# The up projections of a bilinear FFN as 7 block products instead of 8, with 15 block additions on VectorE

## The chip, the cores and the metric

One core of a Trainium2 chip runs the whole program. The metric is the device time of one execution in microseconds (us). The kernel before was run three times: 1170.25, 1170.40 and 1171.97 us, median 1170.4 us.

## The reference

Two stages. A routing attention over 4 batch elements, 8 heads, 768 positions, head size 64: each query and key is put into one of 16 clusters, scores between different clusters are masked, then softmax and a product with `v`. Its output, laid out as 3072 tokens by 512, goes through a bilinear FFN:

```python
x = attn_out.transpose(0, 2, 1, 3).reshape(B * S, H * D)   # 3072 x 512
a = x @ w_a                                                # 512 x 1536
b = x @ w_b                                                # 512 x 1536
return (a * b @ w_out).astype(np.float32)                  # 1536 x 512
```

## The kernel before, in words

Everything is float32 on TensorE except the one-hot masks. The program is one hand-written order of work: `short_path` runs 99 groups `g`, six for each pair of heads (16 pairs `p`, four for each batch element), and each engine takes its instructions in that order. A group does two key tiles of 128: `score` (L405; mask L413 and scores L422 on TensorE, exponential on ScalarE L429), `add_up` of the previous group (L433; row sums `acc`, L443, on VectorE for the first element, later mostly on GpSimd), `weigh` of the previous group (L448; product with `v`, L454), one step of preparing the next pair (`prep_steps`, L378; the assignment to clusters, `prep_assign`, is five VectorE operations from L345 to L356), and every third group `denominators` (L465). Later `normalize` (L483) takes the reciprocals of one half of 384 queries (three VectorE operations, L488) and multiplies `xT` by them on GpSimd (L490).

The FFN runs between, as filler, from the deque `ffn`. `ffn_block` (L502) makes the pieces of one block of 384 tokens (half an element): for each of 12 slices `f` of 128 hidden columns, `piece_a` multiplies the four 128-row chunks of `w_a` with `xT` (L510) and ScalarE copies the result out (L521); `piece_b` does the same with `w_b` and VectorE multiplies the two into `h` (L525). Then three `down` pieces of 12 matmuls of 512 columns (L531), a copy on ScalarE and a store from SP's queue. Each group adds `PER_GROUP` (L564) to a credit, and pieces are taken, at their cost in columns, until it is used up. `ffn_ready` puts a block in when its half is normalized. What is left after group 98 runs without attention beside it (`some_ffn`, L641).

The PSUM pool `ps_m` has three buffers, shared by FFN pieces, `denominators` and the preparation of the next pair; `ps_s` (scores) and `ps_o` (product with `v`) are apart. The weights come in as float64 and are rounded to float32 in 36 parts of 128 x 512 (`round_w`, L245: VectorE, ScalarE and GpSimd), parts 8 to 35 from group 23 on at 1.75 a group (`due`, L572).

Of the kernel before, what the change touches and what calls it, by code (L numbers as in the profile page):

```python
# [8 lines left out]
FP32 = mybir.dt.float32  # L9
# [21 lines left out]
P = 128  # L31
# [4 lines left out]
def kernel(  # L36
# [26 lines left out]
    csb = const.tile([P, D], FP32)  # L63
    nc.scalar.dma_start(out=csb, in_=centroids.rearrange("h c d -> (h c) d"))
# [4 lines left out]
    }  # L69

# [13 lines left out]
    cn = const.tile([P, 2, D], FP32)  # L84

# [4 lines left out]
    def centroids_in():  # L90

        nc.scalar.activation(out=ce, in_=one, func=AF.Sqrt)
        csq = const.tile([P, D], FP32)
# [21 lines left out]
        for a in range(2):  # L115
            nc.vector.tensor_scalar(out=cn[:, a, :], in0=csb,
                                    scalar1=crinv[:, 0:1], scalar2=None,
                                    op0=ALU.mult)
# [19 lines left out]
def short_path(nc, tc, ctx, c, cn, centroids_in, casts, n_far, q, k, v,  # L138
# [26 lines left out]
    denp = pool("denp", 1)  # L165
    xtp = pool("xtp", 2)
    hp_ = pool("hp", 2)
    hap = pool("hap", 2)
# [117 lines left out]
    def centroids_across():  # L286
        ps = ps_m.tile([P, 512], FP32, name="m")
        nc.tensor.transpose(out=ps[:, 0:P], in_=cn.rearrange("p a d -> p (a d)"),
# [52 lines left out]
    def prep_assign(ps):  # L341
        NG = 24
        sim = ps[:, 0:NG * NC].rearrange("p (g c) -> p g c", c=NC)
        mx = small.tile([P, NG], FP32, name="mx")
        nc.vector.tensor_reduce(out=mx, in_=sim, axis=AX.X, op=ALU.max)  # L345
        rk = simp.tile([P, NG, NC], FP32, name="sim")
        nc.vector.tensor_tensor(  # L347
            out=rk, in0=sim, in1=mx[:, :, None].broadcast_to((P, NG, NC)),
            op=ALU.is_ge)
        nc.vector.tensor_tensor(  # L350
            out=rk, in0=rk, in1=rank[:, None, :].broadcast_to((P, NG, NC)),
            op=ALU.mult)
        first = small.tile([P, NG], FP32, name="first")
        nc.vector.tensor_reduce(out=first, in_=rk, axis=AX.X, op=ALU.max)
        oh = oh_all.rearrange("p n (a e) -> p (n a) e", a=2)
        nc.vector.tensor_tensor(  # L356
            out=oh[:, :, 0:NC], in0=rk,
            in1=first[:, :, None].broadcast_to((P, NG, NC)), op=ALU.is_equal)
# [19 lines left out]
    def prep_steps(p):  # L378
# [3 lines left out]
        def both(*fs):  # L382
# [5 lines left out]
            lambda: prep_assign(prep_across(p)),  # L388
# [7 lines left out]
    unchecked = []  # L396
    UPP = 2 * NJ
# [67 lines left out]
    def denominators(p, hf):  # L465
# [3 lines left out]
        terms = [accs.pop((p, hf))]  # L469
# [7 lines left out]
        den = denp.tile([P, HB], FP32, name="den")  # L477
# [22 lines left out]
    ffn = deque()  # L500

    def ffn_block(b, blk):  # L502
# [25 lines left out]
        def down(n):  # L528
            ps = ps_m.tile([P, 512], FP32, name="m")
            for f in range(NF):  # L530
# [3 lines left out]
            y = wtp.tile([P, DM], FP32, name="rest")  # L534
            nc.scalar.copy(out=y, in_=ps)  # L535
            rows = out[b * S:(b + 1) * S, :].rearrange(
                "(p j) n -> p j n", j=NJ)[:, 3 * blk + n, :]
            nc.sync.dma_start(out=rows, in_=y)
# [5 lines left out]

    blocks = {}

    def ffn_ready(b, blk):

        ups, downs = blocks[b, blk] = ffn_block(b, blk)
        if b > 0:  # L550
            ffn.extend(ups + downs)
        elif blk == 0:
            ffn.extend(ups[0:8])
        else:
            ups0, downs0 = blocks[b, 0]
# [8 lines left out]
    PER_GROUP = (2 * NF * NCH * HB + 3 * NF * DM) * 2 // (HP * GPP)  # L564
    EARLY = HP * GPP + 1
# [5 lines left out]
    for i in range(8, len(w_parts)):  # L571
        due.setdefault(23 + int((i - 8) / 1.75), []).append(i)  # L572
# [11 lines left out]
    prep_assign(prep_across(0))  # L584
    for w in (1, 0):
        prep_onehot(0, w)
    for g in range(NG + 3):
# [27 lines left out]
        round_next()  # L615
        if ffn:
# [14 lines left out]
        if g <= EARLY:  # L631
            first, second = 4, 1
        else:
            first, second = 5, 3 if g < NG else 2
# [253 lines left out]
```

## Time and profile before

| | |
|---|---|
| median of three runs | 1170.4 us |
| the profiled execution | 1171.77 us |
| its span, first to last instruction | 1170.0 us |
| mean granted TensorE clock | 0.997 |
| TensorE busy | 1151.0 us, 98% of the span |
| VectorE, ScalarE, GpSimd busy | 396.3, 335.9, 256.1 us |

The profile is one execution. Busy times are sums of instruction durations on an engine; the chain of waits goes back from the last instruction to what released each step; a granted clock of 1.00 is TensorE's 2.4 GHz. Matmul durations are modelled and overlap, so the cost of one is read from the distance between starts.

### The profile page before, as it was taken

Reading aid. Unit: us, or ns where it says so; the run is one execution under the profiler, and the core shown is the slowest. Engines: PE = TensorE matmul, PEld = TensorE weight load, DVE = VectorE, ACT = ScalarE, POOL = GpSimd, SP = SyncE. Lnnn points to the kernel's source line nnn. Section 1 sums busy time; section 2 is a strip of 40 time slices with the busy share of each in tenths; the row PEclk is TensorE's granted clock in tenths of the full one; section 3 lists DMA queues with packets and bytes.
Section 4 is the critical chain, followed back from the end, with each engine's and each line's share of the span. In section 5 each row is a group of like instructions: output and inputs, shape, how many; then the busy total and the mean of one; then the engine's idle time right before and its main releaser. Section 6 shows DMA issues by size and latency. Waiting matters only on the chain.

```text
span 1170.0 us, 11898 instructions
## 1 busy us (share of the span) xinstructions
PE 1151.0 (98%) x4755; PEld 576.3 (49%) x4755; DVE 396.3 (34%) x614; ACT 335.9 (29%) x608; POOL 256.1 (22%) x245
## 2 busy tenths in 40 slices
PE   6999999999999999999999999999999999999998
PEld 3444555555544455544555445554455545554553
DVE  4899777577611212221122212122211221200100
ACT  4666433434223232312223132321322211100000
POOL 1111243444422132222212122121221321000000
PEclk8999999999999999999999999999999999999999
DMA  5322233322102010010101001010000000000000
GB/s 139 101 77 77 90 95 104 99 82 92 47 18 59 18 41 1 12 39 18 41 1 41 9 18 41 1 41 10 32 1 1 1 18 9 1 1 26 1 1 29
DMA packets 60782, 44.91 MB, mean 38 GB/s; under 512 B 48432, under 2 KB 53040, under 8 KB 60720
## 3 DMA queue, kind: packets, MB, share of 16 engines
q1 hardware_dynamic: 59744, 42.21, 12.5%
q10 hardware_dynamic: 976, 1.87, 0.5%
q8 instruction: 39, 0.64, 0.2%
q14 instruction: 23, 0.19, 0.1%
HBM read 37.78 MB, written 6.29 MB: 38 GB/s over the span
## 4 chain that ended last, share of the span: by engine, by line
PE 94%; DVE 4%; issue 1%; POOL 1%; DMA 0%; ACT 0%; DVEq 0%; POOLq 0%; ACTq 0%
PE m L510 41%; PE m L531 21%; PE O L454 11%; PE s L422 10%; PE s L413 3%; PE m L474 3%; PE m L309 2%; PE m L325 1%; PE m L366 1%; PE m L336 1%; DVE den L488 0%; DVE acc L443 0%; DVE sim L347 0%; DVE mx L345 0%; POOL wo_sb L269 0%
## 5 line engine op out<-in xcount | busy, mean ns | idle before, releaser
L510 PE MATMUL m<-xT,wa_sb 128*128 128x384 f32 x768 | 265.0, 488 | 1.3 <-ACT ohT L371 0.9
L510 PE MATMUL m<-xT,wb_sb 128*128 128x384 f32 x768 | 265.6, 489 | 0.0
L531 PE MATMUL m<-wo_sb,h 128*128 128x512 f32 x576 | 251.9, 595 | 0.0
L443 POOL TENSOR_TENSOR acc<-acc,pt 128x384 f32<-128x384 f32 x144 | 146.8, 1033 | 266.9 <-ACT pt L429 263.2
L525 DVE TENSOR_TENSOR h<-ha,m 128x384 f32<-128x384 f32 x96 | 53.2, 554 | 443.1 <-PE m L510 443.1
L510 PEld LDWEIGHTS m<-xT,wb_sb 128*128 128x128 f32 x768 | 143.9, 190 | 107.1 <-issue 9.6
L510 PEld LDWEIGHTS m<-xT,wa_sb 128*128 128x128 f32 x768 | 143.7, 190 | 105.4 <-issue 7.1
L429 ACT ACTIVATE pt<-s 128x768 f32<-128x768 f32 x192 | 145.3, 809 | 109.3 <-PE s L422 72.6
L531 PEld LDWEIGHTS m<-wo_sb,h 128*128 128x128 f32 x576 | 108.0, 190 | 137.1 <-issue 135.4
L521 ACT COPY ha<-m 128x384 f32<-128x384 f32 x96 | 45.9, 478 | 366.9 <-PE m L510 366.9
L454 PE MATMUL O<-pt,v 128*64 128x384 f32 x768 | 144.8, 499 | 0.0
L422 PE MATMUL s<-qkT 64*128 64x384 f32 x768 | 140.8, 486 | 0.0
L443 DVE TENSOR_TENSOR acc<-acc,pt 128x384 f32<-128x384 f32 x96 | 76.7, 828 | 158.9 <-POOL acc L443 158.5
L490 POOL TENSOR_TENSOR xT<-xT,den 128x384 f32<-128x384 f32 x32 | 33.8, 1057 | 255.6 <-DVE den L488 241.0
L454 PEld LDWEIGHTS O<-pt,v 128*64 128x64 f32 x768 | 46.6, 136 | 86.5 <-issue 84.1
L422 PEld LDWEIGHTS s<-qkT 64*128 64x128 f32 x768 | 71.1, 189 | 32.0 <-issue 0.6
L535 ACT COPY rest<-m 128x512 f32<-128x512 f32 x24 | 14.1, 585 | 250.3 <-PE m L531 250.3
L488 DVE RECIPROCAL den<-den 128x128 f32<-128x128 f32 x96 | 82.2, 911 | 3.6 <-ACT den L479 3.5
L413 PE MATMUL s<-ohT 64*128 64x384 bf16 x384 | 48.2, 329 | 0.7 <-DVE ohT L374 0.7
L443 DVE TENSOR_TENSOR acc<-pt 128x384 f32<-128x384 f32 x40 | 30.2, 772 | 51.7 <-ACT pt L429 51.7
L443 POOL TENSOR_TENSOR acc<-pt 128x384 f32<-128x384 f32 x24 | 27.2, 1134 | 45.7 <-ACT pt L429 45.7
L309 PE MATMUL m<-ident,qk 128*128 128x128 f32 x192 | 28.5, 289 | 6.7 <-DVE nfar L281 6.7
(84 smaller groups left out, 507.0 us busy)
## 6 DMA issues: line engine op xcount, KB each, us to landing
raw<-in_moe_w_out_dram SPq DMA_DIRECT2D x12, 512.0 KB, 3.2
out_dram<-rest SPq DMA_DIRECT2D x24, 256.0 KB, 2.0
qk<-in_q_dram SPq DMA_DIRECT2D x30, 192.0 KB, 3.8
qk<-in_k_dram SPq DMA_DIRECT2D x30, 192.0 KB, 4.1
v<-in_v_dram SPq DMA_DIRECT2D x15, 384.0 KB, 4.3
raw<-in_moe_w_a_dram SPq DMA_DIRECT2D x11, 512.0 KB, 3.5
raw<-in_moe_w_b_dram SPq DMA_DIRECT2D x11, 512.0 KB, 3.5
raw<-in_moe_w_a_dram ACTq DMA_DIRECT2D x1, 512.0 KB, 4.2
```

What stands on the lines that cost most here:

```text
L309: nc.tensor.transpose(out=ps[:, n * P:(n + 1) * P], in_=qks[p][:, w, j].rearrange("p a d -> p (a d)"), identity=ident)
L413: nc.tensor.matmul(out=s[:, a, 0:HB], lhsT=ohTs[p][r, S + j * P:S + (j + 1) * P], rhs=ohTs[p][r, hf * HB:(hf + 1) * HB], start=True, stop= ...
L422: nc.tensor.matmul(out=s[:, a, 0:HB], lhsT=qkTs[p][r, S + j * P:S + (j + 1) * P], rhs=qkTs[p][r, hf * HB:(hf + 1) * HB], start=False, stop ...
L429: nc.scalar.activation(out=pt, in_=s[:, :, 0:HB], func=AF.Exp, scale=SCALE)
L443: eng.tensor_tensor(out=acc[:, a, :], in0=probs[u - 1][:, a, :] if j == 1 else acc[:, a, :], in1=probs[u][:, a, :], op=ALU.add)
L454: nc.tensor.matmul(out=O_of[0][a * D:(a + 1) * D, 0:HB], lhsT=vs[p][:, a, j, :], rhs=probs[u][:, a, :], start=(j == 0), stop=(j == NJ - 1))
L474: nc.tensor.matmul(out=ps[a * D:(a + 1) * D, 0:HB], lhsT=ones, rhs=t[:, a, :], start=(n == 0), stop=(n == len(terms) - 1))
L488: nc.vector.reciprocal(out=part, in_=part)
L510: nc.tensor.matmul(out=ps[:, 0:HB], lhsT=w_sb[:, ch, f * P:(f + 1) * P], rhs=xTs[b][:, ch, t0:t0 + HB], start=(ch == 0), stop=(ch == NCH - 1))
L521: nc.scalar.copy(out=box["a"], in_=ps[:, 0:HB])
L525: nc.vector.tensor_tensor(out=box["h"][:, f, :], in0=box["a"], in1=ps[:, 0:HB], op=ALU.mult)
L531: nc.tensor.matmul(out=ps, lhsT=box["h"][:, f, n * P:(n + 1) * P], rhs=wo_sb[:, f, :], start=(f == 0), stop=(f == NF - 1))
```

## The change

For batch elements 1 to 3 both up projections are done by one level of Strassen's algorithm in the form with 15 additions. The 512 rows of `xT` and the 1536 hidden columns are each cut in two, and so are the 768 tokens; where eight block products stood there are seven. For each slice `i` of 6 and each of `w_a`, `w_b` there is a set: seven products `p1`, `p6`, `p2`, `p7`, `p4`, `p5`, `p3` of two matmuls each (128 x 128 weights, 384 tokens), four combinations S1 to S4 of weight blocks (eight VectorE operations of 128 x 128, in `half_1` and `half_2`), a copy of `p1` on ScalarE and seven VectorE additions that read PSUM. Four combinations of `xT` blocks (`combine_x`, eight VectorE operations of 128 x 384 per element) are made when the halves are normalized, one of them in place. The product with `a` moves to GpSimd (`done`, four per `w_b` set). Work space is that of the weight rounding, which is over by then. Element 0 keeps `ffn_block`.

Around it: a `todo` deque spreads the five operations of `prep_assign` and the three reciprocals of `normalize` between FFN pieces, one behind each; `normalize` stands ahead of the pieces of its group and `ffn_ready` behind them; the reciprocals are taken in `acc[:, 0, :]` and not in a tile of their own; the credit is 3813 a group until group 51 and 4224 after, where it was 4608; parts of the weight rounding fall due at 1.5 a group. An element's FFN now waits for both of its halves, so that of element 3 begins behind group 98. The centroids' tiles at the start lie in room of `wo_sb`, with the same instructions. The `down` pieces are as before.

```diff
-    denp = pool("denp", 1)
     xtp = pool("xtp", 2)
     hp_ = pool("hp", 2)
-    hap = pool("hap", 2)
+    hap = pool("hap", 3)
...
             both(lambda: prep_transpose(p, 0), lambda: prep_transpose(p, 1)),
             both(lambda: prep_sim(p), lambda: load_v(p)),
-            lambda: prep_assign(prep_across(p)),
+            lambda: todo.extend(prep_assign(prep_across(p))),
...
-        terms = [accs.pop((p, hf))]
+        acc = accs.pop((p, hf))
+        terms = [acc]
...
-        den = denp.tile([P, HB], FP32, name="den")
+        den = acc[:, 0, :]
...
         b, hp = divmod(p, HP)
         den = den_of.pop((p, hf))
-        for n in range(3):
+        x = xTs[b][:, hp, hf * HB:(hf + 1) * HB]
+
+        def invert(n):
             part = den[:, n * P:(n + 1) * P]
             nc.vector.reciprocal(out=part, in_=part)
-        x = xTs[b][:, hp, hf * HB:(hf + 1) * HB]
-        nc.gpsimd.tensor_tensor(out=x, in0=x, in1=den, op=ALU.mult)
-        unchecked.append((4 * p + 2 * hf + 1, den))
+
+        def apply():
+            nc.gpsimd.tensor_tensor(out=x, in0=x, in1=den, op=ALU.mult)
+            unchecked.append((4 * p + 2 * hf + 1, den))
+
+        return [lambda n=n: invert(n) for n in range(3)] + [apply]
...
+    def winograd_room():
+        raw = [rawp.tile([P, 2 * WN], FP32, name="raw") for _ in range(2)]
+        size = [sizep.tile([P, WN], FP32, name="size") for _ in range(2)]
+        quarter = lambda t: t[:, 0:2 * HB].rearrange("p (c t) -> p c t", c=2)
+        beside = lambda t: t[:, 2 * HB:].rearrange("p (c f) -> p c f", c=2)
+        chunks = lambda t: [t[:, c, :] for c in range(2)]
+        W["T3"], W["T2"] = chunks(quarter(raw[0])), chunks(quarter(raw[1]))
+        W["T4"] = [t[:, 0:HB] for t in size]
+        more = combp.tile([P, 2, P], FP32, name="comb")
+        W["slots"] = [chunks(beside(raw[0])), chunks(beside(raw[1])),
+                      chunks(more), [t[:, HB:] for t in size]]
...
+    def combine_x(b, c):
+
+        if not W:
+            winograd_room()
+        x = xTs[b]
+        x11, x12 = x[:, c, 0:HB], x[:, c, HB:S]
+        x21, x22 = x[:, c + 2, 0:HB], x[:, c + 2, HB:S]
+        for out, in0, in1 in ((W["T3"][c], x22, x12), (x12, x12, x11),
+                              (W["T2"][c], x22, x12), (W["T4"][c], W["T2"][c], x21)):
+            nc.vector.tensor_tensor(out=out, in0=in0, in1=in1, op=ALU.subtract)
...
+    def ffn_winograd(b):
+
+        h = []
+        x = xTs[b]
+        X = {"11": [x[:, c, 0:HB] for c in (0, 1)],
+             "T1": [x[:, c, HB:S] for c in (0, 1)],
+             "21": [x[:, c, 0:HB] for c in (2, 3)],
+             "22": [x[:, c, HB:S] for c in (2, 3)],
+             "T2": W["T2"], "T3": W["T3"], "T4": W["T4"]}
+
+        def products(w_sb, i, is_a):
+            N2 = NF // 2
+            A = {m + n: [w_sb[:, c, f * P:(f + 1) * P] for c in cs]
+                 for m, f in (("1", i), ("2", i + N2))
+                 for n, cs in (("1", (0, 1)), ("2", (2, 3)))}
+            box = {}
+
+            def combine(name, l, r, op):
+
+                at = {"S1": 1, "S2": 2, "S3": 0, "S4": 3}[name]
+                dst = W["slots"][at]
+                for c in range(2):
+                    nc.vector.tensor_tensor(out=dst[c], in0=l[c], in1=r[c], op=op)
+                A[name] = dst
+
+            def half_1():
+                combine("S1", A["21"], A["22"], ALU.add)
+                combine("S2", A["S1"], A["11"], ALU.subtract)
+
+            def half_2():
+                combine("S3", A["11"], A["21"], ALU.subtract)
+                combine("S4", A["12"], A["S2"], ALU.subtract)
+                s = W["slots"]
+                W["slots"] = [s[1], s[2], s[0], s[3]]
+
+            def product(l, r):
+                ps = ps_m.tile([P, 512], FP32, name="m")
+                for c in range(2):
+                    nc.tensor.matmul(out=ps[:, 0:HB], lhsT=A[l][c], rhs=X[r][c],
+                                     start=(c == 0), stop=(c == 1))
+                return ps[:, 0:HB]
+
+            def place(k, f):
+                if is_a:
+                    return h[k][:, f, :]
+                return hap.tile([P, HB], FP32, name="ha")
+
+            def add(out, in0, ps, op=ALU.add):
+                nc.vector.tensor_tensor(out=out, in0=in0, in1=ps, op=op)
+
+            def done(name, k, f):
+                if not is_a:
+                    to = h[k][:, f, :]
+                    nc.gpsimd.tensor_tensor(out=to, in0=to, in1=box[name],
+                                            op=ALU.mult)
+
+            def p1():
+                if not h:
+                    h.extend(hp_.tile([P, NF, HB], FP32, name="h")
+                             for _ in range(2))
+                ps = product("11", "11")
+                box["11"] = place(0, i)
+                nc.scalar.copy(out=box["11"], in_=ps)
+
+            def p6():
+                ps = product("S2", "T2")
+                box["12"] = place(1, i)
+                add(box["12"], box["11"], ps)
+
+            def p2():
+                add(box["11"], box["11"], product("12", "21"))
+                done("11", 0, i)
+
+            def p7():
+                ps = product("S3", "T3")
+                box["22"] = place(1, i + N2)
+                add(box["22"], box["12"], ps)
+
+            def p4():
+                ps = product("22", "T4")
+                box["21"] = place(0, i + N2)
+                add(box["21"], box["22"], ps, ALU.subtract)
+                done("21", 0, i + N2)
+
+            def p5():
+                ps = product("S1", "T1")
+                add(box["12"], box["12"], ps)
+                add(box["22"], box["22"], ps)
+                done("22", 1, i + N2)
+
+            def p3():
+                add(box["12"], box["12"], product("S4", "22"))
+                done("12", 1, i)
+
+            return half_1, half_2, [p1, p6, p2, p7, p4, p5, p3]
+
+        def down(k, n):
+            ps = ps_m.tile([P, 512], FP32, name="m")
+            for f in range(NF):
+                nc.tensor.matmul(out=ps, lhsT=h[k][:, f, n * P:(n + 1) * P],
+                                 rhs=wo_sb[:, f, :],
+                                 start=(f == 0), stop=(f == NF - 1))
+            store(b, 3 * k + n, ps)
+
+        def both(*fs):
+            return lambda: [f() for f in fs]
+
+        parts = [products(w_sb, i, w_sb is wa_sb) for i in range(NF // 2)
+                 for w_sb in (wa_sb, wb_sb)]
+        pieces = []
+        for n, (half_1, half_2, ps) in enumerate(parts):
+            ps[0] = both(*([half_1] if n == 0 else []), half_2, ps[0])
+            if n + 1 < len(parts):
+                ps[4] = both(ps[4], parts[n + 1][0])
+            pieces += [(2 * HB, f) for f in ps]
+        return pieces + [(NF * DM, lambda k=k, n=n: down(k, n))
...
     blocks = {}
 
-    def ffn_ready(b, blk):
-
-        ups, downs = blocks[b, blk] = ffn_block(b, blk)
+    def ffn_ready(p, hf):
+
+        b, hp = divmod(p, HP)
         if b > 0:
-            ffn.extend(ups + downs)
-        elif blk == 0:
+            if (hp, hf) == (2, 1):
+                combine_x(b, 0)
+            elif (hp, hf) == (3, 1):
+                combine_x(b, 1)
+                ffn.extend(ffn_winograd(b))
+        elif (hp, hf) == (3, 0):
+            ups, downs = blocks[0] = ffn_block(0, 0)
             ffn.extend(ups[0:8])
...
-            ups0, downs0 = blocks[b, 0]
+        elif (hp, hf) == (3, 1):
...
-    PER_GROUP = (2 * NF * NCH * HB + 3 * NF * DM) * 2 // (HP * GPP)
-    EARLY = HP * GPP + 1
+
+
+    BG = HP * GPP
+    PER_GROUP = [(2 * NF * ups * HB + 6 * NF * DM) // n
+                 for ups, n in ((2 * NCH, BG + 5), (7 * NCH // 4, BG))]
...
     for i in range(8, len(w_parts)):
-        due.setdefault(23 + int((i - 8) / 1.75), []).append(i)
+        due.setdefault(23 + int((i - 8) / 1.5), []).append(i)
...
+        ph = {first: (p, 0), second: (p - 1, 1)}.get(l)
+        halved = ph in den_of
+        if halved:
+            todo.extend(normalize(*ph))
         if ffn:
-            credit += PER_GROUP
+            credit += PER_GROUP[g > 2 * BG + 3]
             while ffn and credit > 0:
                 cost, piece = ffn.popleft()
                 credit -= cost
                 piece()
+                if todo:
+                    todo.popleft()()
                 round_next()
         else:
             credit = 0
         round_next()
+        while todo:
+            todo.popleft()()
+        if halved:
+            ffn_ready(*ph)
```

## Rows read from the trace of the kernel before

**Rows 1.** The page, busy time of each engine over the span:
```profile
PE 1151.0 (98%) x4755; PEld 576.3 (49%) x4755; DVE 396.3 (34%) x614; ACT 335.9 (29%) x608; POOL 256.1 (22%) x245
```

**Rows 2.** The page, chain that ended last, shares by engine and by line:
```profile
PE 94%; DVE 4%; issue 1%; POOL 1%; DMA 0%; ACT 0%; DVEq 0%; POOLq 0%; ACTq 0%
PE m L510 41%; PE m L531 21%; PE O L454 11%; PE s L422 10%; PE s L413 3%; PE m L474 3%; PE m L309 2%; PE m L325 1%; PE m L366 1%; PE m L336 1%; DVE den L488 0%; DVE acc L443 0%; DVE sim L347 0%; DVE mx L345 0%; POOL wo_sb L269 0%
```

**Rows 3.** The page, groups (line, engine, operation, shapes, count | busy, mean | idle before, releaser):
```profile
L510 PE MATMUL m<-xT,wa_sb 128*128 128x384 f32 x768 | 265.0, 488 | 1.3 <-ACT ohT L371 0.9
L510 PE MATMUL m<-xT,wb_sb 128*128 128x384 f32 x768 | 265.6, 489 | 0.0
L531 PE MATMUL m<-wo_sb,h 128*128 128x512 f32 x576 | 251.9, 595 | 0.0
L443 POOL TENSOR_TENSOR acc<-acc,pt 128x384 f32<-128x384 f32 x144 | 146.8, 1033 | 266.9 <-ACT pt L429 263.2
L525 DVE TENSOR_TENSOR h<-ha,m 128x384 f32<-128x384 f32 x96 | 53.2, 554 | 443.1 <-PE m L510 443.1
L521 ACT COPY ha<-m 128x384 f32<-128x384 f32 x96 | 45.9, 478 | 366.9 <-PE m L510 366.9
L488 DVE RECIPROCAL den<-den 128x128 f32<-128x128 f32 x96 | 82.2, 911 | 3.6 <-ACT den L479 3.5
```

**Rows 4.** Busy time in four stretches (mean granted clock, DMA share, GB/s at the end):
```profile
0.00:120.00 120.00, 107.35 (x688) 50.12 (x690) 96.69 (x165) 68.70 (x120) 20.86 (x23) 0.97 0.37 100
120.00:300.00 180.00, 178.71 (x771) 94.26 (x768) 130.23 (x200) 67.56 (x122) 70.70 (x62) 1.00 0.32 96
300.00:960.00 660.00, 660.00 (x2701) 324.30 (x2701) 147.67 (x215) 177.84 (x321) 156.29 (x153) 1.00 0.07 20
977.80:1170.00 192.20, 187.15 (x535) 100.29 (x534) 16.50 (x31) 16.57 (x35) 1.84 (x2) 1.00 0.02 9
```

**Rows 5.** The chain in order of time (start, us, what), its last two pieces:
```profile
1072.13 61.92 PE m L510 x192
1134.05 30.91 PE m L531 x72
```

**Rows 6.** Timeline from the last attention group on (start, us, engine, what):
```profile
977.74 2.85 PE L510 MATMUL m<-xT,wa_sb 128*128 128x384 f32 x8
1004.63 2.74 PE L510 MATMUL m<-xT,wa_sb 128*128 128x384 f32 x8
1004.90 0.55 DVE L525 TENSOR_TENSOR h<-ha,m 128x384 f32<-128x384 f32 x1 [2.12 <-PE m L510]
1007.21 2.74 PE L510 MATMUL m<-xT,wb_sb 128*128 128x384 f32 x8
```

**Rows 7.** Timeline of attention work and of VectorE and GpSimd, 481 to 492 us:
```profile
481.82 0.50 PE L413 MATMUL s<-ohT 64*128 64x384 bf16 x4
482.15 1.45 PE L422 MATMUL s<-qkT 64*128 64x384 f32 x8
482.47 2.57 DVE L488 RECIPROCAL den<-den 128x128 f32<-128x128 f32 x3
483.54 1.51 PE L454 MATMUL O<-pt,v 128*64 128x384 f32 x8
486.14 3.21 POOL L443 TENSOR_TENSOR acc<-acc,pt 128x384 f32<-128x384 f32 x3
487.16 1.34 DVE L443 TENSOR_TENSOR acc<-acc,pt 128x384 f32<-128x384 f32 x1 [2.13 <-POOL acc L443]
491.81 0.55 DVE L443 TENSOR_TENSOR acc<-pt 128x384 f32<-128x384 f32 x1
```

**Rows 8.** Timeline of VectorE and GpSimd, 311 to 314 us:
```profile
311.35 3.23 POOL L443 TENSOR_TENSOR acc<-acc,pt 128x384 f32<-128x384 f32 x3
312.68 0.56 DVE L525 TENSOR_TENSOR h<-ha,m 128x384 f32<-128x384 f32 x1 [2.17 <-PE m L510]
```

**Rows 9.** Groups of VectorE by form: a small operation with two SBUF inputs:
```profile
L95 DVE TENSOR_TENSOR csq<-csb 128x64 f32<-128x64 f32 x1 | 0.2, 226 | 2.8 <-DMA csb<-in_centroids_dram 2.8
```

More of the change, by code (lines that the diff above doesn't have):

```diff
@@ L69 @@
     }
+    room = c["wo_sb"][:, 0, :]
+    csb, csq, cn = room[:, 0:D], room[:, D:2 * D], room[:, 2 * D:4 * D]
+    nc.scalar.dma_start(out=csb, in_=centroids.rearrange("h c d -> (h c) d"))
     one = const.tile([P, 1], FP32)
@@ L82 @@
     rank = c["rank"] = const.tile([P, NC], FP32, name="rank")
-    cn = const.tile([P, 2, D], FP32)
     def casts():
@@ L343, in prep_assign @@
         sim = ps[:, 0:NG * NC].rearrange("p (g c) -> p g c", c=NC)
+        shape = (P, NG, NC)
         mx = small.tile([P, NG], FP32, name="mx")
-        nc.vector.tensor_reduce(out=mx, in_=sim, axis=AX.X, op=ALU.max)
         rk = simp.tile([P, NG, NC], FP32, name="sim")
[L347 to L352, printed above, removed]
         first = small.tile([P, NG], FP32, name="first")
-        nc.vector.tensor_reduce(out=first, in_=rk, axis=AX.X, op=ALU.max)
         oh = oh_all.rearrange("p n (a e) -> p (n a) e", a=2)
-        nc.vector.tensor_tensor(
-            out=oh[:, :, 0:NC], in0=rk,
-            in1=first[:, :, None].broadcast_to((P, NG, NC)), op=ALU.is_equal)
+        top = lambda t: t[:, :, None].broadcast_to(shape)
+        v = nc.vector
+        return [
+            lambda: v.tensor_reduce(out=mx, in_=sim, axis=AX.X, op=ALU.max),
+            lambda: v.tensor_tensor(out=rk, in0=sim, in1=top(mx), op=ALU.is_ge),
+            lambda: v.tensor_tensor(
+                out=rk, in0=rk, in1=rank[:, None, :].broadcast_to(shape),
+                op=ALU.mult),
+            lambda: v.tensor_reduce(out=first, in_=rk, axis=AX.X, op=ALU.max),
+            lambda: v.tensor_tensor(out=oh[:, :, 0:NC], in0=rk, in1=top(first),
+                                    op=ALU.is_equal),
+        ]
     def prep_onehot(p, w):
@@ L396, in short_path @@
     unchecked = []
+    todo = deque()
     UPP = 2 * NJ
@@ L500, in short_path, with store @@
     ffn = deque()
+    def store(b, j, ps):
+        y = wtp.tile([P, DM], FP32, name="rest")
+        nc.scalar.copy(out=y, in_=ps)
+        rows = out[b * S:(b + 1) * S, :].rearrange("(p j) n -> p j n", j=NJ)
+        nc.sync.dma_start(out=rows[:, j, :], in_=y)
     def ffn_block(b, blk):
@@ L533, in down @@
                                  start=(f == 0), stop=(f == NF - 1))
[L534 to L538, printed above, removed]
+            store(b, 3 * blk + n, ps)
         ups = [(NCH * HB, lambda f=f, piece=piece: piece(f))
@@ L543, in ffn_block @@
         return ups, downs
+    W = {}
+    def winograd_room():
[9 more added lines that the diff above has]
+                      chunks(more), [t[:, HB:] for t in size]]
@@ new lines, in combine_x @@
+    def combine_x(b, c):
[102 more added lines that the diff above has]
+        return pieces + [(NF * DM, lambda k=k, n=n: down(k, n))
+                         for k in range(2) for n in range(3)]
@@ L553, in ffn_ready @@
             ffn.extend(ups[0:8])
-        else:
-            ups0, downs0 = blocks[b, 0]
+        elif (hp, hf) == (3, 1):
+            ups0, downs0 = blocks[0]
+            ups, downs = ffn_block(0, 1)
             for n in range(3):
@@ L583, in short_path @@
     prep_sim(0)
-    prep_assign(prep_across(0))
+    for step in prep_assign(prep_across(0)):
+        step()
     for w in (1, 0):
@@ L615, in short_path @@
         round_next()
+        if g <= EARLY:
+            first, second = 4, 1
+        else:
+            first, second = 5, 3 if g < NG else 2
+        ph = {first: (p, 0), second: (p - 1, 1)}.get(l)
+        halved = ph in den_of
+        if halved:
+            todo.extend(normalize(*ph))
         if ffn:
-            credit += PER_GROUP
+            credit += PER_GROUP[g > 2 * BG + 3]
             while ffn and credit > 0:
@@ L630, in short_path @@
             prep_onehot(p + 1, 0)
[L631 to L634, printed above, removed]
-        ph = {first: (p, 0), second: (p - 1, 1)}.get(l)
-        if ph in den_of:
-            normalize(*ph)
-            if ph[0] % HP == HP - 1:
-                ffn_ready(ph[0] // HP, ph[1])
     def some_ffn(n):
```

9 lines of the change are left out of this document (4 added, 5 removed).

## The prediction

> **What bounds the kernel now.** Read the busy shares first [rows 1]: TensorE is busy 98% of the span, the next engine, VectorE, 34%. Busy matmul time alone proves little, since matmuls overlap, so the chain of waits comes next [rows 2]: 94% of what ended last is TensorE, and the up projection's line L510 is 41% by itself; VectorE holds 4%. The groups [rows 3] show the same from the other side: before the up projections, `down` and the rest there is next to no idle time with a releaser, while VectorE and ScalarE wait hundreds of us for L510. Then the stretches [rows 4]: from 300 to 960 us TensorE is busy 660.00 of 660 us, VectorE 147.67 (22%) and GpSimd 156.29 (24%). Only in the first 120 us is it otherwise: VectorE is at 96.69 of 120 us and TensorE has gaps. No Strassen work is put there. The granted clock is 1.00 from 120 us on, so durations are those of the 2.4 GHz level.
>
> The price of an up-projection matmul is read where nothing is beside it: in the chain by time [rows 5], 192 matmul records of L510 fill 61.92 us without a gap, 322.5 ns each. Starts of neighbouring pieces of eight records are 2.58 us apart [rows 6], the same number, so the shown 488 ns [rows 3] is overlap. The code has 8 blocks x 12 slices x 4 chunks = 384 matmuls for each projection and the row has 768, so one matmul is two records: 645 ns.
>
> **What is removed.** For one batch element the two projections are 2 blocks x 24 pieces x 8 = 384 records. After: 12 sets x 7 products x 2 matmuls x 2 records = 336. That is 48 fewer for each of three elements, 144 in all, x 322.5 ns = **46.4 us off TensorE**. `down`, attention and element 0 keep theirs. Since TensorE sets the end, all of this comes off, less what TensorE newly waits.
>
> **What is added.** Per set, VectorE does seven additions that read PSUM and one SBUF operand. The row nearest to them is L525, same shape and sources: 0.554 us [rows 3]. Then eight weight combinations, 128 x 128, two SBUF operands. No row has that shape; the ends are 0.23 us for 64 columns [rows 9] and 0.55 us for 384 [rows 7]. A line through both gives 0.29 us at 128, which I take. Sum for a set: 7 x 0.55 + 8 x 0.29 = 6.2 us of VectorE beside 28 x 0.3225 = 9.03 us of TensorE. Even at the upper end (8 x 0.55) it is 8.3 us and VectorE keeps up. For 36 sets this is 223 us; with 24 `xT` combinations at 0.55 (13 us) and without 72 multiplications of L525 (40 us), VectorE goes from 396 to about 590 us, half of the span. GpSimd gets 72 multiplications at 1.03 us [rows 3] = 74 us, to about 330. ScalarE has 36 copies of `p1` where it had 72 of `ha`, 17 us less. Averages thus leave TensorE as the bound; the price can only be in bursts.
>
> **The wait that could come.** A product takes 1.29 us of TensorE and a PSUM buffer of three. The product three places on starts 2.58 us after this one's end, so VectorE may be late by 2.58 - 0.55 - about 0.1 = 1.9 us before TensorE stops. Behind `p4`'s addition VectorE has `half_1` (4 x 0.29 = 1.2 us) and then two additions for `p5`; behind `p3`'s it has `half_2`. Without GpSimd, `p5`'s buffer comes free some 1.7 us after its end: no stop. In a `w_b` set GpSimd multiplies (1.03 us) just as `half_1` starts. What two engines cost each other is in the trace: VectorE's `acc` addition, two SBUF operands, takes 0.55 us alone and 1.34 us when GpSimd is at it [rows 7], +0.79; L525, with one operand in PSUM, takes 0.56 us in the midst of three GpSimd additions [rows 8], +0. So the seven additions are not slowed, and the combinations are. With one GpSimd operation in the way, `p5`'s buffer comes about 0.8 to 1.1 us later, 2.5 to 2.8 us after its end, some 0.25 us too late at worst. At 18 `w_b` sets that is 0 to 4.5 us; GpSimd's operation lies there in every such set, so I take two thirds: **+3 us**.
>
> **Middle groups.** For elements 1 and 2 the products lie between attention groups, 5 or 6 a group by the new credit (4224 / 768), in some 31 groups. VectorE has per group 5.5 x 6.2 / 7 = 4.9 us, an `acc` addition (0.55 to 1.34), on average 0.9 us of reciprocals and 0.5 us of `prep_assign` (five operations of 0.56 in one group of six): up to 7.6 us. TensorE has 5.5 x 1.29 = 7.1 us of products and 0.50 + 1.45 + 1.51 us of attention [rows 7], over 10.5 us. In a group with three reciprocals (2.57 us [rows 7]) the products' phase is overfull by about 1 us, which the 1.9 us above take up and the 3.5 us of attention give back, since that work uses other PSUM pools. Taken as nothing; without this cover it would be 1 us in most of the 31 groups (a rival below).
>
> **What is moved.** An element's FFN begins only when both halves are normalized. The chain there is reciprocals 2.6, multiplication on GpSimd 1.0, four combinations of `xT` 2.2, `half_1` and `half_2` 2.3 us: 8.1 us. Counting the credit through, a whole `down` piece (24 x 0.43 = 10.3 us, [rows 5]: 30.91 / 72) stands in TensorE's queue in the group before or in the same group each time, the last in group 98, and VectorE can run ahead of it. So nothing. `den` in `acc` makes one `acc` addition in six groups wait for ScalarE's check, some 3.5 us into the group, while TensorE does its attention share: nothing, and behind it on VectorE stand only the first additions of the group. `ffn_ready` now comes ahead of the next pair's transposes; it issues VectorE work only, and no DMA is moved past on SP's or GpSimd's queue. Weight parts at 1.5 a group still land a group before their first use, as 1.75 did with the faster credit. With 3813 of credit, element 0's groups shrink by about half a piece, 1.3 us of TensorE, and VectorE (130.23 of 180 us there [rows 4]) has fewer parts in each: nothing to +10 us, nothing taken.
>
> **Sum.** 1171.77 (the profiled execution; span 1170.0 plus 1.8) - 46.4 + 3.0 = 1128.4 us. The median of the runs lies 1.4 us under the profiled one, so **1127.0 us**, 3.7% faster. A measurement of this kernel can tell about 0.2% (2.3 us) from no change.
>
> **Rivals.**
>
> *Bursts reach TensorE.* In the 31 middle groups `todo`, the combinations and GpSimd's three `acc` additions (3.21 us [rows 7]) come together, and TensorE waits 0.7 us in each: 22 us, so 1149, between 1135 and 1160. For: VectorE waits for GpSimd's `acc` already now. Against: the order within a group puts 3.5 us of attention before the first product.
>
> *VectorE becomes the bound, slower.* If every combination finds GpSimd at work it costs 0.29 + 0.79, a set 3.85 + 8 x 1.08 = 12.5 us beside 9.03; TensorE waits 3.5 x 36 = 125 us and the time is 1127 - 3 + 125 = 1249. It decides from (9.03 + 46.4 / 36 - 6.2) / 0.79 = 5.2 of 8 combinations hit in every set. For: +0.79 is real [rows 7]. Against: GpSimd would be busy 330 of 1127 us, and behind the attention it has only four operations in two sets.
> The Trainium skill ("SBUF — State Buffer", section "Who interferes with whom") says more than a slow-down: a VectorE instruction with two SBUF inputs and a GpSimd instruction that reads SBUF exclude each other, and the later one blocks fully until the first is done; by it this rival happens wherever GpSimd's queue is dense. The trace agrees on the pairing (0.55 against 1.34 us, and 0.56 with PSUM), and what it gives at GpSimd's present density is the +3 us above.
>
> *Short products cost a start each.* If a product of four records paid the 0.11 us that a first piece shows over a later one (2.85 us behind attention work against 2.74 [rows 6]), 252 products give 28 us: 1155. Against: pieces of eight records change PSUM bank with no gap at all [rows 6].
>
> *The slower credit lets the weight rounding through.* TensorE waits 0.5 us in each of 19 groups of element 0's FFN: 1137.
>
> *It isn't what it says.* If the program had more than 336 records for an element, the gain would go with the count; 28 x 12 is plain in the code, so no chance of its own.
>
> **Chances.** Forecast (1124 to 1132) 0.66; bursts 0.18; slow credit 0.06; starts 0.05; VectorE bound 0.05, nearly all of it slower. The range reaches from 1121 (no new wait, and the 1.3 us of gaps between 120 and 300 us [rows 4] and some spread of the runs gained too) to 1147, which takes in the slow credit and the lower half of the bursts: about 0.81. Faster by over 0.2%: 0.93; within 0.2%: 0.03; slower: 0.04.
>
> **What would show it.** After the change: 1008 records of product matmuls at 322.5 ns in the stretch behind the attention, about 108 us for element 3's products; seven PSUM additions at 0.55 us a set whatever GpSimd does; combinations at 0.29 us, some at 1.1. TensorE's waits name VectorE's combinations or GpSimd for a few us only. If the span between 330 and 960 us has TensorE under 99%, bursts have won; if behind the attention a set takes over 9.5 us, VectorE is late there too. A time over 1147 or under 1121 makes the prediction wrong.

## The result, and the profile after

The changed kernel takes 1131.01 us (median of 4 runs, 1129.34 to 1132.29) against 1170.46; the ratio is 0.9659, 95% interval 0.9643 to 0.9676: 39.5 us or 3.4% faster. Forecast were 1127.0 us, range 1121 to 1147. Its profiled execution took 1132.29 us, span 1130.6.

The page's busy times and the first lines of its chain, of the kernel after (those before are in [rows 1] and [rows 2]):

```profile
PE 1106.9 (98%) x4611; PEld 549.1 (49%) x4611; DVE 612.2 (54%) x1106; ACT 319.9 (28%) x572; POOL 333.8 (30%) x317
...
PE 91%; DVE 6%; issue 1%; POOL 1%; ACT 1%; DMA 0%; DVEq 0%; ACTq 0%
PE m L625 26%; PE m L686 17%; PE m L526 11%; PE O L457 11%; PE s L425 10%; PE m L547 6%; PE s L416 3%; PE m L478 3%; PE m L308 2%; PE m L324 1%; PE m L368 1%; DVE raw L609 1%; DVE ha L635 1%; POOL h L640 1%; DVE size L609 1%
```

TensorE has 4755 - 4611 = 144 records fewer, as counted, and is busy 98% still. Products are L625, `down` of elements 1 to 3 is L686. New in the chain are VectorE's combinations (L609) and additions (L635) and GpSimd's multiplications (L640): somewhere TensorE now waits for them. The view of TensorE's waits says where, and the stretches say in which part of the program (columns as in [rows 4]; the last one is element 3's products behind the attention):

```profile
PE m L308 <- DVE nfar L280: 6.5, 1, 6.5
PE m L368 <- DVE oh L358: 3.2, 1, 3.2
PE m L625 <- DVE sim L353: 2.6, 2, 1.3
PE m L625 <- DVE comb L609: 2.2, 2, 1.1
PE m L478 <- DVE acc L446: 1.6, 4, 0.4
PE s L416 <- DVE ohT L376: 0.6, 1, 0.6
PE m L335 <- ACT sim L329: 0.6, 1, 0.6
PE m L625 <- DVE h L635: 0.5, 2, 0.2
```

```profile
120.00:300.00 180.00, 180.00 (x800) 94.15 (x798) 131.32 (x200) 70.09 (x125) 74.05 (x65) 1.00 0.31 94
300.00:960.00 660.00, 654.25 (x2667) 316.90 (x2666) 313.00 (x571) 172.22 (x311) 214.96 (x205) 1.00 0.08 22
967.68:1063.33 95.65, 95.65 (x297) 56.43 (x298) 65.93 (x156) 4.79 (x10) 22.09 (x23) 1.00 0.00 1
```

Behind the attention nothing is lost: TensorE is busy 95.65 us of 95.65, and the 296 product records that start there are 323 ns apart. Between 120 and 300 us the 1.3 us of gaps before are gone. All that is newly lost, 5.75 us of idle TensorE, lies in the middle, and each of the two long waits (for L353 and for L609) comes once for element 1 and once for element 2. The waits of the first 120 us (L308, L368, L478, L416, L335) were there before the change too.

The first long wait, in the timeline where element 1's products begin:

```profile
425.74 1.45 PE L425 MATMUL s<-qkT 64*128 64x384 f32 x8
426.68 1.51 ACT L432 ACTIVATE pt<-s 128x768 f32<-128x768 f32 x2 [0.68 <-PE s L425]
428.07 0.52 ACT L506 ACTIVATE acc<-acc 128x384 f32<-128x384 f32 x1
428.72 0.56 DVE L446 TENSOR_TENSOR acc<-pt 128x384 f32<-128x384 f32 x1 [7.26 <-ACT acc L506]
428.77 1.38 POOL L446 TENSOR_TENSOR acc<-pt 128x384 f32<-128x384 f32 x1 [9.68 <-ACT acc L506]
429.20 2.10 DVE L609 TENSOR_TENSOR raw<-wa_sb 128x128 f32<-128x128 f32 x2
429.80 1.56 PE L625 MATMUL m<-xT,wa_sb 128*128 128x384 f32 x4
430.10 3.25 POOL L446 TENSOR_TENSOR acc<-acc,pt 128x384 f32<-128x384 f32 x3
431.22 1.28 DVE L609 TENSOR_TENSOR comb<-raw,wa_sb 128x128 f32<-128x128 f32 x2
432.44 1.53 PE L625 MATMUL m<-raw,comb 128*128 128x384 f32 x4 [1.09 <-DVE comb L609]
433.62 0.48 DVE L609 TENSOR_TENSOR size<-wa_sb,comb 128x128 f32<-128x128 f32 x2
```

VectorE is idle for 7.26 us because its next instruction, an `acc` addition, waits for ScalarE's check of the reciprocals (L506), which stands behind two exponentials. Only then come S1 and S2, and these meet GpSimd: 2.10 us for a pair that takes 0.48 us alone (the last line). S2 (`comb`) is 1.09 us too late for `p6`.

The second, in the group with the cluster assignment:

```profile
546.99 0.54 DVE L635 TENSOR_TENSOR ha<-ha,m 128x384 f32<-128x384 f32 x1
547.46 0.55 DVE L352 TENSOR_REDUCE mx<-m 128x24 f32<-128x384 f32 x1
547.89 0.99 POOL L640 TENSOR_TENSOR h<-h,ha 128x384 f32<-128x384 f32 x1
547.92 2.11 DVE L609 TENSOR_TENSOR comb<-wa_sb 128x128 f32<-128x128 f32 x2
548.85 3.25 POOL L446 TENSOR_TENSOR acc<-acc,pt 128x384 f32<-128x384 f32 x3
549.96 1.28 DVE L609 TENSOR_TENSOR size<-wa_sb,raw 128x128 f32<-128x128 f32 x2
551.16 0.54 DVE L353 TENSOR_TENSOR sim<-m,mx 128x384 f32<-128x384 f32 x1
551.63 0.54 DVE L635 TENSOR_TENSOR h<-h,m 128x384 f32<-128x384 f32 x1
551.85 1.53 PE L625 MATMUL m<-raw,comb 128*128 128x384 f32 x4 [1.30 <-DVE sim L353]
```

`p7` waits for a PSUM buffer that the assignment still holds: its second operation (L353) has been spread behind a piece, and now stands behind four combinations, 3.2 us, which GpSimd holds up: the first by its multiplication with `a` (L640), the next two by the first two of its three additions. Those additions belong to the next group: GpSimd does them as soon as the exponentials are done, and so beside the products.

### The profile page after: what moved, and what is told of

It reads as the page before. It is cut to its first block, busy times and chain, and to the rows that moved or that the text cites. A ratio compares the mean times of both kernels' runs of the same rounds, so it can differ in the third digit from the quotient of the medians.

```text
span 1130.6 us, 12198 instructions
## 1 busy us (share of the span) xinstructions
PE 1106.9 (98%) x4611; PEld 549.1 (49%) x4611; DVE 612.2 (54%) x1106; ACT 319.9 (28%) x572; POOL 333.8 (30%) x317
## 4 chain that ended last, share of the span: by engine, by line
PE 91%; DVE 6%; issue 1%; POOL 1%; ACT 1%; DMA 0%; DVEq 0%; ACTq 0%
PE m L625 26%; PE m L686 17%; PE m L526 11%; PE O L457 11%; PE s L425 10%; PE m L547 6%; PE s L416 3%; PE m L478 3%; PE m L308 2%; PE m L324 1%; PE m L368 1%; DVE raw L609 1%; DVE ha L635 1%; POOL h L640 1%; DVE size L609 1%
## 5 line engine op out<-in xcount | busy, mean ns | idle before, releaser
L686 PE MATMUL m<-wo_sb,h 128*128 128x512 f32 x432 | 188.1, 594 | 0.0
L640 POOL TENSOR_TENSOR h<-h,ha 128x384 f32<-128x384 f32 x72 | 72.7, 1017 | 263.1 <-DVE ha L635 229.2
L446 DVE TENSOR_TENSOR acc<-acc,pt 128x384 f32<-128x384 f32 x96 | 82.3, 886 | 95.5 <-POOL acc L446 95.1
L686 PEld LDWEIGHTS m<-wo_sb,h 128*128 128x128 f32 x432 | 81.3, 190 | 102.6 <-issue 99.6
L635 DVE TENSOR_TENSOR ha<-ha,m 128x384 f32<-128x384 f32 x126 | 66.5, 545 | 87.4 <-PE m L625 87.2
L635 DVE TENSOR_TENSOR h<-h,m 128x384 f32<-128x384 f32 x126 | 66.9, 544 | 69.0 <-PE m L625 68.5
L495 DVE RECIPROCAL acc<-acc 128x128 f32<-128x128 f32 x96 | 85.9, 924 | 12.0 <-ACT acc L483 12.0
L625 PE MATMUL m<-raw 128*128 128x384 f32 x192 | 70.3, 489 | 0.0
L498 POOL TENSOR_TENSOR xT<-xT,acc 128x384 f32<-128x384 f32 x32 | 33.0, 1030 | 124.4 <-DVE acc L495 109.8
L526 PE MATMUL m<-xT,wb_sb 128*128 128x384 f32 x192 | 66.7, 490 | 0.0
L526 PE MATMUL m<-xT,wa_sb 128*128 128x384 f32 x192 | 66.5, 489 | 0.0
L625 PE MATMUL m<-xT,wa_sb 128*128 128x384 f32 x144 | 53.2, 492 | 0.5 <-DVE h L635 0.5
```

Source lines behind the costliest of these rows:

```text
L446: eng.tensor_tensor(out=acc[:, a, :], in0=probs[u - 1][:, a, :] if j == 1 else acc[:, a, :], in1=probs[u][:, a, :], op=ALU.add)
L526: nc.tensor.matmul(out=ps[:, 0:HB], lhsT=w_sb[:, ch, f * P:(f + 1) * P], rhs=xTs[b][:, ch, t0:t0 + HB], start=(ch == 0), stop=(ch == NCH - 1))
L625: nc.tensor.matmul(out=ps[:, 0:HB], lhsT=A[l][c], rhs=X[r][c], start=(c == 0), stop=(c == 1))
L635: nc.vector.tensor_tensor(out=out, in0=in0, in1=ps, op=op)
L640: nc.gpsimd.tensor_tensor(out=to, in0=to, in1=box[name], op=ALU.mult)
L686: nc.tensor.matmul(out=ps, lhsT=h[k][:, f, n * P:(n + 1) * P], rhs=wo_sb[:, f, :], start=(f == 0), stop=(f == NF - 1))
```

## The experiments

All edits are against the changed kernel unless said otherwise. Theory at first: 46.4 us are saved, some 4.5 are lost again in those waits, 2.4 by the reordering. Rival: VectorE's load costs something in every set.

**1. The reordering alone.**

```diff
-                combine_x(b, 1)
-                ffn.extend(ffn_winograd(b))
+                ups0, downs0 = ffn_block(b, 0)
+                ups1, downs1 = ffn_block(b, 1)
+                ffn.extend(ups0 + ups1 + downs0 + downs1)
...
```

The credit after group 51 is again that of eight products, 4608, here and in run 2.

> Elements 1 to 3 go back to the eight-product FFN pieces, both blocks of an element queued together; everything else of the change stays (todo, den in acc, the credit of element 0, due times, both halves awaited). My theory: the arithmetic saving is 144 records x 322.5 ns = 46.4 us, and of the 7 us that are missing about 4.5 are TensorE waits at a few places that only the products have, so the reordering by itself costs at most 2.4 us: 1170 to 1173 us. Rival: the reordering (longer wait for both halves, slower credit, check of den) is where the 7 us went: 1176 or more, and the products then give all 46.

Measured: 1168.92 us, ratio 0.9987 (0.9977 to 0.9996). The reordering costs nothing; it gives 1.6 us. Both expectations were off; the products and additions thus cost more than the theory had, 1131.0 - (1168.9 - 46.4) = 8.5 us.

**2. Products for element 3 only.**

```diff
-        if b > 0:
+        if 0 < b < 3:
+            if (hp, hf) == (3, 1):
...
+        elif b == 3:
             if (hp, hf) == (2, 1):
                 combine_x(b, 0)
...
```

> As the run before, but element 3, whose FFN runs behind the attention, keeps the seven products. Theory: 48 fewer records x 322.5 ns, no wait behind the attention: 15.5 us under the reordering alone, 1154.5 to 1157.5 us, and a product stretch of about 108 us without gaps. Rival (VectorE's load costs a little in every set): each of the 12 sets loses some 0.2 us, so 12 to 13 us under the reordering alone.

1153.33 us, 15.6 under run 1 (48 x 322.5 ns = 15.5). Behind the attention the additions are free; the rival falls there.

**3. No weight combinations.**

```diff
-                for c in range(2):
-                    nc.vector.tensor_tensor(out=dst[c], in0=l[c], in1=r[c], op=op)
-                A[name] = dst
+                A[name] = l
```

> The 288 weight combinations of VectorE are left out: products use the plain weight blocks in the places of S1 to S4. TensorE's records are the same. Theory: the two waits of 1.08 us where an element's products begin vanish, and the two of 1.30 us beside the cluster assignment too, since there GpSimd-blocked combinations stand ahead of the operation that frees the PSUM buffer: about 1126.5 us, 4 to 5 under the changed kernel. Rival (VectorE's load in every set): 7 us or more, 1124 us or less. If combinations cost TensorE nothing: 1131.

1122.98 us: 45.9 under run 1, so the matmul price holds, and 8.0 under the changed kernel, as the rival said. But not in every set. Both programs have the same stretches of FFN work on TensorE in the same order, so the lag of one behind the other can be followed by the start of each:

```
lag added, us                      element 1     element 2
start of products                    1.33          1.31
a group with reciprocals             0.39          0.37
two more groups, reciprocals         0.81 + 0.10   0.82 + 0.09
group with the assignment            1.53          1.54
all other groups, and element 3      0             0
```

The sum is 8.3 us: the theory's places, 1.7 times the 4.8 us of its four waits. The waits view shows only idle time, counted from the modelled end of a product, and without a wait the next one starts some 0.24 us before that end (lags of 1.33 and 1.53 us against waits of 1.09 and 1.30); and the theory left out the groups with reciprocals.

**4. Every combination twice.**

```diff
-                for c in range(2):
+                for c in (0, 0, 1, 1):
```

> Every weight combination is written twice: 288 more VectorE operations of 0.28 us alone and up to 1.1 us beside GpSimd. Theory: behind the attention a set needs 7 x 0.55 + 16 x 0.28 = 8.3 us of VectorE against 9.03 us of TensorE and still fits (under 3 us lost there, by GpSimd's blocking); in the middle the places that wait now wait about twice as long: 1136 to 1142 us. Rival (VectorE is already at its limit in the products): each of 36 sets loses the added 2.2 us or most of it, 1160 to 1210 us.

1172.67 us, 41.7 more and no faster than the kernel before (ratio 1.0015, 1.0004 to 1.0027). This is the rival's size, but not its place. By starts of stretches 42.2 us are lost against run 3 up to the end of the attention and 6.7 behind it, and 37.8 of the 42.2 lie in the five places of the table above, where the changed kernel loses 8.3. VectorE is thus not at its limit in every set; but in those places twice the combinations cost TensorE 4.6 times as much, and not twice as the theory had it. An estimated 8.7 us of that are the clock's (last section).

**5. The first set's combinations one group earlier.**

```diff
-            ps[0] = both(*([half_1] if n == 0 else []), half_2, ps[0])
+            if n == 0:
+                half_1()
+                half_2()
+            else:
+                ps[0] = both(half_2, ps[0])
```

> The eight combinations of an element's first set are issued when its second half is ready (behind combine_x), not one group later behind that group's acc addition. Beside the kernel without combinations the changed kernel lags by 1.33 us at each of the two starts of products between attention groups. Theory (S2 is late because it stands on VectorE behind an acc addition that waits for ScalarE's check, and is then blocked by GpSimd): both lags vanish, 2.7 us, 1128.3 us. Rival (S2 is late by GpSimd's blocking alone, wherever it stands, or p6 waits for something else): under 1 us.

1127.54 us, ratio 0.9631 (0.9618 to 0.9644). Both lags at the start of products are gone, the others stand unchanged to 0.02 us.

**6. The check ahead of the exponentials.**

```diff
+        check_inverses()
         if g < NG:
             score(now)
-        check_inverses()
```

> The check of the reciprocals on ScalarE is issued ahead of a group's scores, so that its two exponentials no longer stand before it; nothing else is moved. Theory (the acc addition waits for that check because den now lies in acc): VectorE's addition at the start of an element's products comes some 3 us earlier and the two lags of 1.33 us vanish: 1128.3 us. Rival (the check is not what is late, GpSimd's blocking is): no change, 1131 us, or slower if the exponentials now wait for GpSimd's multiplication of xT.

1134.15 us, slower. Yet both lags at the start of products vanish here too: the check, late since `den` lies in `acc`, is what made S2 late. The price is elsewhere: before the first FFN piece, where exponentials wait for the check and scores for exponentials (TensorE's waits: `s` L416 for ACT `pt`, 5.2 us in six). That piece starts 3.7 us later than in the changed kernel, 1.0 more than the two lags give back. The medians differ by 3.1: the profiled execution was the fastest of five here and the slowest of four there, and the traces show no other cause.

**7. The assignment's first two operations at once.**

```diff
-            lambda: todo.extend(prep_assign(prep_across(p))),
+            lambda: assign_begin(p),
```

(`assign_begin` runs two of the five steps and puts three into `todo`.)

> The first two operations of the cluster assignment, those that read its PSUM buffer, are issued at once instead of one behind each FFN piece. Theory (p7 of that group waits for the buffer, which the second operation frees only behind GpSimd-blocked combinations): the two lags of 1.53 us, one for each of elements 1 and 2, vanish: 1128 us. Rival (VectorE is simply overfull in that group, whatever the order): the lag stays, as a wait for another addition, 1130.5 to 1132 us.

1130.22 us. The wait for L353 shrinks from 2.6 to 0.7 us in total and one for an addition (L635) grows from 0.5 to 2.2: that group's lag is 1.75 instead of 1.53. Only the lag of 0.38 us in the first group with reciprocals is gone, and the interval of the ratio (0.9641 to 0.9667) takes in the changed kernel's 0.9659. The rival is right so far: in either of these two orders VectorE has too much to do in that group.

**8. Runs 5 and 7 together.**

> The first set's combinations early and the assignment's first two operations at once. Theory: both kinds of lag vanish, 2 x (1.33 + 1.53) = 5.7 us, 1125.3 us, faster than both kernels; what is left over the kernel without combinations is 2.6 us in the groups with reciprocals. Rival (overfull VectorE): under 3 us, 1128.5 us or more.

1127.62 us, no better than run 5 alone: moving the two operations gives nothing, as the rival of run 7 has it, and 5.7 us were not to be had this way. What makes the group overfull, VectorE's own work or its waiting for GpSimd, was left; the next four kernels start from run 5.

**9. S4 later.**

```diff
-                combine("S4", A["12"], A["S2"], ALU.subtract)
...
+            def half_3():
+                combine("S4", A["12"], A["S2"], ALU.subtract)
...
+            ps[2] = both(ps[2], half_3)
```

> On top of the early first set (1127.5 us): S4, needed only by the last product of a set, is combined behind p2's addition and no longer with S3 ahead of p1. Left over the kernel without combinations are 5.7 us in four groups of each of elements 1 and 2 (0.4 and 0.9 us with reciprocals, 1.5 us with the cluster assignment). Theory (a pair of GpSimd-blocked combinations, 1.3 us, stands ahead of the operations that free PSUM buffers): the assignment's 1.5 us shrink to a few tenths, 2 to 4 us in all, 1123.5 to 1125.5 us. Rival (VectorE is overfull in those groups by the sum of its work): the wait moves to a later product, 1127 us or more.

1123.97 us, ratio 0.9599 (0.9586 to 0.9612), 3.6 under run 5. The assignment's lag is 0.33 us, and the waits view lists no wait for VectorE in a product; 2.3 us of lag against run 3 are left in all. So order does count, when a blocked pair, and not two free operations, is moved.

**10. The multiplications on VectorE.**

```diff
-                    nc.gpsimd.tensor_tensor(out=to, in0=to, in1=box[name],
+                    nc.vector.tensor_tensor(out=to, in0=to, in1=box[name],
```

> On top of the early first set: the 72 multiplications of the FFN's two halves go from GpSimd (1.02 us each) to VectorE (0.55 us, two SBUF operands), so GpSimd has only attention work. Theory (what blocks is GpSimd's acc additions of the next group, which it does beside the products): they still block, VectorE has 40 us more, and the lags grow, 1131 to 1140 us. Rival (the multiplications, which fall in just ahead of combinations, are what blocks): 1122 to 1126 us.

1124.61 us, 2.9 under run 5: VectorE gets 72 more operations and is later nowhere but in one group of each element (0.75 us). Its busy time even falls, from 606 us in run 5 to 604. The theory was wrong to name one piece of GpSimd's work as the only one that blocks: in run 5 47 of the 288 combinations take over 0.9 us, here 8, and in run 12, where the additions into `acc` are gone instead, 31.

**11. The combinations on GpSimd.**

```diff
-                    nc.vector.tensor_tensor(out=dst[c], in0=l[c], in1=r[c], op=op)
+                    nc.gpsimd.tensor_tensor(out=dst[c], in0=l[c], in1=r[c], op=op)
```

> On top of the early first set: the 288 weight combinations go from VectorE to GpSimd. VectorE then has 3.85 us a set. If GpSimd keeps up, TensorE's lags vanish and the time is that without combinations, 1122 to 1124 us. Against it: GpSimd takes about twice as long for an operation (1.03 us against 0.55 at 384 columns), and behind its acc additions (3.2 us a group) S2 and S3 come late. I expect late ones to win: TensorE waits for GpSimd in many of the 31 groups, 1135 to 1160 us.

1123.06 us, ratio 0.9586 (0.9573 to 0.9599): the best here, clear of the changed kernel's interval though not of run 9's, and the time without any combinations (1122.98). My expectation was wrong. Its busy times, and one of GpSimd's groups of combinations (min, median, max in ns):

```profile
PE 1103.8 (98%) x4611; PEld 549.1 (49%) x4611; DVE 520.9 (46%) x818; ACT 319.6 (29%) x572; POOL 461.2 (41%) x605
```

```profile
L609 POOL TENSOR_TENSOR raw<-wa_sb x48: 448/456/772, 418.4 to 1039.5; 128x128 f32<-128x128 f32 x48
```

GpSimd needs 0.456 us for one, not the 1.0 of a 384-column operation, and 41% busy it keeps up; no product waits for anything.

**12. No `acc` additions on GpSimd.**

```diff
             many = p >= HP and (a == 1 or j in (2, 4))
+            if many and j > 1:
+                continue
```

> On top of the early first set: GpSimd's 144 additions into acc are left out (the softmax sums then lack those terms); VectorE's part of the sums, the multiplications on GpSimd and everything on TensorE stay. Theory (these additions, done a group ahead, hold the VectorE combinations up): the four lags of each element vanish, 5.7 us, 1121.5 to 1123 us. Rival (VectorE is overfull by its own work): 1126 us or more.

1122.54 us. Three of the four lags vanish, one of 0.46 us stays. VectorE does the same work here as in run 5 and is busy 562 us, not 606: some 44 us of its busy time there were waiting beside GpSimd's additions, more than half of it in VectorE's own `acc` additions (113.9 us there, 89.3 here). With runs 9 and 10 that answers runs 7 and 8: the groups were overfull by GpSimd, not by VectorE's own work. What it does not separate: in run 5 VectorE also sits idle for GpSimd's additions, since its own continue their sums (95 us in all; in the changed kernel 2.08 us ahead of the second long wait), and this idle time goes with the additions. In run 10 the additions stay, and 80 us of this idle time with them, and two of the four lags vanish even so.

Not tried: `den` in a tile of its own, and `acc` additions on VectorE that do not continue GpSimd's sums.

## Why the prediction was right, and which of its steps failed

**The bound and the saving: right.** TensorE ends the kernel before and after; 144 records at 322.5 ns are 46.4 us, measured 45.9 (run 3 against run 1) and 15.6 of 15.5 for one element (run 2).

**The prices of VectorE: right.** A combination takes 0.28 us alone (0.29 was drawn between two rows), a PSUM addition 0.545 whatever GpSimd does; the slowest combinations take 1.11 (0.29 + 0.79 = 1.08 was the rival's price). GpSimd is busy 333.8 us (330 forecast), VectorE 612.2 where 590 were summed: the combinations take 100 us of it (512.3 in run 3) where 84 were summed, and its `acc` additions 7 us more than before the change.

**"+3 us" for `p5`'s buffer: size too small, place wrong.** The term was set on all 18 `w_b` sets. Element 3's six lose nothing at all. There the one GpSimd multiplication that the step counted on lies beside `half_1` as it said, and no buffer comes late. What the combinations cost is 8.0 us, all of it beside attention.

**"Middle groups: taken as nothing" failed.** It counted VectorE's work in a group at its price alone, 7.6 us, and let 1.9 us of PSUM slack and the attention's share take up the bursts. In the groups with reciprocals or the assignment GpSimd's additions for the next group, and a multiplication just ahead of them, lie beside the products, and two pairs of combinations then take up to 3.4 us instead of 1.0. This is the burst rival in kind, at 5.6 us instead of 22; the prediction's own sign for it, TensorE under 99% between 330 and 960 us, was just not met (624.25 of 630 us, 99.1%).

**"`den` in `acc` ... nothing" failed**, twice 1.3 us. The wait was seen, but it was said that only the group's first additions stand behind it; at the start of an element `half_1` does too, and S2 is wanted by the second product. Where the step counted a `down` piece as cover, the cover held for `combine_x`, which was done 0.8 us before the scores of group 51. But group 51 itself has no pieces, so nothing covered `half_1`, which is issued a group later.

**"What is moved: nothing", for the rest, held**: it gave 1.6 us (run 1), of which 1.3 are the gaps between 120 and 300 us that the range's lower end had in it.

Together: 1170.5 - 46.4 - 1.6 + 8.0 = 1130.5, measured 1131.0; the other 0.5 is 45.9 in place of 46.4. That the sum came within 4 us is in part luck: its 3 us stood for a wait of `p5` that the waits view does not show, the 8.0 us came from two steps taken as nothing, and the 1.6 us gained made up for some of them. The bound VectorE of the slower rival was not met: over 0.9 us take 54 of 288 combinations, 1.5 of 8. But its deciding point (5.2 of 8 in every set, 4.1 us more of VectorE in each) was an average where bursts decide: 2.2 us more in a set (run 4) already ate the whole gain.

## What to carry to other kernels

A cheaper algorithm on the bounding engine is paid for in the places where the helper's queue is already full, not in its average load: list for each group of the schedule what stands ahead of the operation that frees a buffer or makes an operand. Price the helper's operations beside what its neighbour does at that moment, next group's work included. And where two engines block each other, give one of them the whole kind of operation that collides: that was worth as much as leaving the operations out.

## What the runs showed of the hardware

*Blocking is per operation.* In the second long wait, three of VectorE's four combinations each wait for one GpSimd operation and then go through, the first for the multiplication, two for additions, and the fourth passes at 0.28 us: 2.11 us for two, 1.28 for the next two. The slowest of the changed kernel's 288 took 1.11 us, so a dense GpSimd queue did not hold VectorE for longer than one operation at a time. The Trainium skill ("SBUF — State Buffer", section "Who interferes with whom") calls the shared port pair an exclusive lock, which the second of the two engines has to wait for; the trace agrees, with one operation as the unit (1.05 us a combination against 0.28 alone, and 0.54 for an addition from PSUM beside the same GpSimd additions).

*The granted clock fell at TensorE's longest waits.* In run 4, with the combinations twice, these are two stretches in each of elements 1 and 2 (columns as in [rows 4]) and the four longest waits of its products:

```profile
510.00:540.00 30.00, 25.91 (x105) 13.59 (x104) 21.02 (x42) 6.35 (x11) 12.24 (x12) 0.94 0.00 1
540.00:570.00 30.00, 25.88 (x110) 12.79 (x110) 19.51 (x43) 5.62 (x10) 10.04 (x10) 0.94 0.17 40
810.00:840.00 30.00, 26.16 (x107) 13.50 (x108) 18.94 (x42) 7.45 (x15) 8.15 (x8) 0.89 0.04 13
840.00:870.00 30.00, 25.87 (x100) 13.07 (x100) 23.26 (x54) 4.46 (x7) 9.04 (x9) 0.94 0.00 1
```

```profile
530.32 2.00 PE L625 MATMUL m<-xT,wa_sb 128*128 128x384 f32 x4 [3.52 <-DVE h L635]
565.08 2.56 PE L625 MATMUL m<-raw,comb 128*128 128x384 f32 x4 [3.34 <-DVE sim L353]
819.59 2.93 PE L625 MATMUL m<-xT,wa_sb 128*128 128x384 f32 x4 [3.53 <-DVE h L635]
855.25 2.59 PE L625 MATMUL m<-raw,comb 128*128 128x384 f32 x4 [3.35 <-DVE sim L353]
```

TensorE is busy 25.9 to 26.2 of 30 us there, and the mean granted clock is 0.89 to 0.94. The clock falls to the lower level of 1.2 GHz four times in this part, once at each of these four waits, in the wait or just behind it, and records of products then start 0.64 us apart instead of 0.32. None of the shorter waits of its products had a fall. In the changed kernel, whose products wait at most 1.30 us, TensorE is busy 28.7 of 30 us or more in the same stretches, and the clock stays at 1.00. By the four clocks shown, 30 x (0.06 + 0.06 + 0.11 + 0.06) = 8.7 us are lost in run 4 beyond the waits themselves, an estimate. So these four waits cost more than their own length.
